# Premultiplied q and k weights in chunks of six whole heads, each matrix transposed in six transfers

## The chip, the cores and the metric

The kernel runs on one NeuronCore of a Trainium2 chip. The core has TensorE (PE: matrix multiply, writing to the eight banks of PSUM), VectorE (DVE), ScalarE (ACT), GpSimd (POOL) and SyncE (SP, here only a queue that starts DMAs). The engines run side by side, each through its own queue in order, and wait for each other through semaphores. The metric is the device time of one execution in microseconds (us), as the median of several runs.

## The reference

For 2,048 tokens of width 640 it computes a gated mixture of two branches of the same input x. Branch A is a linear attention with 32 heads of 20 features, where softmax feature maps stand in for the attention matrix; branch B is a SwiGLU feed-forward network with 1,728 hidden features.

```
g = sigmoid((x * gate_w).sum(-1, keepdims=True))
q, k, v = heads of x @ wqkv
pq = einsum("bhsd,hdf->bhsf", q, w_phi)      # pk the same from k
phi_q = concat([softmax(pq), softmax(-pq)])  # phi_k the same from pk
kv = einsum("bhsf,bhsd->bhfd", phi_k, v)
z = einsum("bhsf->bhf", phi_k)
a = (einsum("bhqf,bhfd->bhqd", phi_q, kv) / (einsum("bhqf,bhf->bhq", phi_q, z) + 1e-6)) @ wo
b = (silu(x @ w_gate) * (x @ w_up)) @ w_down
out = g * a + (1 - g) * b
```

All inputs are bfloat16.

## The kernel before

Since pq = (x @ wq) @ w_phi head by head, the kernel multiplies the weights first: it forms wq' = wq @ blockdiag(w_phi) and wk' likewise, two matrices of 640 x 640, once per execution. After that each tile of 128 tokens needs one product with wq' or wk' (tile `wqk`) instead of two.

This premultiplication is what the change touches. For the matmul, the weights must lie with their output features on the partitions, so a DMA transpose brings the q and the k part of `A_wqkv` into SBUF transposed, as tile `wqT` (`load_wT`, one transfer for each matrix). w_phi is loaded into `wph`, and POOL builds the block diagonal matrices `wbd` out of it (`build_wbd`: a copy repeated for each head, then two selections that clear what lies off the diagonal blocks). `premult` then takes five groups for each matrix, one for each 128 rows of the result: six matmuls, an eviction by ACT or DVE into `wqk`. The 640 columns are cut into five chunks of 128 there, and as 128 is not a multiple of 20, a head can straddle two chunks. A chunk covers all heads that it touches (`PHI_H0`, `PHI_NH`: 7, 7, 8, 7 and 7 heads, 720 columns for 640), the straddling heads are summed in PSUM, and the middle chunk is cut in two, so that each half of the result fills 320 columns of its own bank.

The order of the work is not written out by hand. Every piece of work is a task with an estimated cost, dependences, a priority and sometimes a time before which it may not start. A planner (`_Plan.run`) plays these tasks through when the program is built and so fixes the order on each engine; the chip then executes that order, with real waits on semaphores. Loads have a due time (`land`) in this plan and are chained, so that SP issues them in the order of the source. What reads a load is planned no earlier than its due time (with a slack of 1.0 for the later loads). The order around the change on SP's queue is: x for tokens 512 to 1023, w_phi, a piece of the gate and of the up weights, the transposed k weights, another piece of both, the v weights, x for tokens 1024 to 1535, two more pieces of both, x for the last 512 tokens, the transposed q weights, then w_down and wo. On TensorE, the first tiles of the FFN come first; the groups for k are spread between FFN tiles from 24 us on, the value products (`vtile`) and key products (`ktile`) of the first tokens follow, and the groups for q lie between FFN work from 45 us on. In the later part, FFN, query tiles (`qtile`) and the down projection are interleaved.

Of the kernel before, what the change touches and what calls it, by code (L numbers as in the profile page):

```python
# [6 lines left out]
P = 128  # L7
S_TOK = 2048
D = 640
H = 32  # L10
DH = 20
F_FFN = 1728
# [10 lines left out]
OW = HP * DH  # L23
KV_G = (0, 6, NG)

PHI_H0 = (0, 6, 12, 19, 25)
PHI_NH = (7, 7, 8, 7, 7)
ACTF = mybir.ActivationFunctionType
ALU = mybir.AluOpType
AX = mybir.AxisListType  # L30
# [1 line left out]
BF16 = DT.bfloat16  # L32
# [204 lines left out]
class _Plan:  # L237
# [11 lines left out]
    def add(self, eng, cost, fn, deps=(), prio=5.0, lat=None, acq=(), rel=(), name=""):  # L249
        t = _Task(eng, cost, fn, deps, prio, self.LAT[eng] if lat is None else lat,  # L250
                  tuple(acq), tuple(rel), len(self.tasks), name)
        self.tasks.append(t)
        return t
# [86 lines left out]
def _build(  # L340
# [13 lines left out]
    pe, act, dve, pool, sp = nc.tensor, nc.scalar, nc.vector, nc.gpsimd, nc.sync  # L354
# [13 lines left out]
    def sbat(name, shape, dtype, at):  # L368
        t = nc.alloc_sbuf_tensor_at(name, list(shape), dtype, offset=at)
        tr.reg_tensor(t, "sbuf", at, rowelems(shape), mybir.dt.size(dtype))  # L370
        return t

    xT = sb("xT", [P, 5, S_TOK], BF16)
    wqk = sb("wqk", [P, 2, 5, D], BF16)
    wvg = sb("wvg", [P, 5, D + 1], BF16)
    wo = sb("wo", [P, 5, D], BF16)
    wd = sb("wd", [P, NK, D], BF16)
    wg = sb("wg", [P, 5, F_FFN + 64], BF16)
# [24 lines left out]
    base = nc.lookup_mloc(slab).addr  # L403
    assert base % 32 == 0, base
    xsb = sbat("xsb", [P, NT, D], BF16, base)
    wqT = sbat("wqT", [P, 10, D], BF16, base)
    wbd = sbat("wbd", [P, 5, 8, DH], BF16, base + 10 * D * 2)
    wph = sbat("wph", [P, 5, DH], BF16, base + 10 * D * 2 + 5 * 8 * DH * 2)

    ps = nc.alloc_psum_tensor("ps", [P, 8 * 512], F32)  # L410
    tr.addr[ps.name] = ("psum", 0, 8 * 512, 4)
# [5 lines left out]
    add = plan.add  # L417

    def bank(i, j, c0, c1, r0=0, r1=P):
        return ps[r0:r1, (2 * i + j) * 512 + c0:(2 * i + j) * 512 + c1]  # L420
# [4 lines left out]
    def wide(i, n=D):  # L425
        return ps[:, 2 * i * 512:2 * i * 512 + n]

    def mms(groups):

        reads = [g[1] for g in groups] + [g[2] for g in groups]  # L430
        writes = []
        seen = set()
        for g in groups:
            k = (g[0].offset, str(g[0].ap))
            if k not in seen:
                seen.add(k)
                writes.append(g[0])

        def fn():
            last = None  # L440
            for o, l, r, st, sp_ in groups:
                last = pe.matmul(o, lhsT=l, rhs=r, start=st, stop=sp_, skip_group_check=True)  # L442
            return last
        run("pe", fn, reads=reads, writes=writes)
# [12 lines left out]
    def poolop(fn, reads, writes):  # L457
        run("pool", fn, reads=reads, writes=writes)

    def memset(t_ap, val, eng):  # L460
        eobj = {"pool": pool, "dve": dve}[eng]
        run(eng, lambda: eobj.memset(t_ap, val), reads=[], writes=[t_ap])
# [23 lines left out]
    def load(eng, dst, src, land, prio, transpose=False, name="load", cost=0.06):  # L486

        t = add(eng, cost, lambda: dma(eng, dst, src, transpose=transpose), prio=prio, lat=2.0, name=name)
        t.land = land
        t.slack = L_SLACK if land > 13 else 0.0  # L490
        t.after = chain.get(eng)
        chain[eng] = t
        return t

    def rows(a):
        return a.rearrange("(c p) j -> p c j", p=P)
    gsrc = rows(B_w_gate)
    usrc = rows(B_w_up)
    PIECES = ((0, 512), (512, 768), (768, 1024), (1024, 1344), (1344, 1664))
    NPC = len(PIECES)  # L500
    wgl = [None] * (NPC + 1)
    wul = [None] * (NPC + 1)

    def load_gu(j, eng, land, prio):
        c0, c1 = PIECES[j]
        wgl[j] = load(eng, wg[:, :, c0:c1], gsrc[:, :, c0:c1], land[0], prio)
        wul[j] = load(eng, wu[:, :, c0:c1], usrc[:, :, c0:c1], land[1], prio + 0.1)

    def load_x(bt, prio, *cuts):

        tok = slice(512 * bt, 512 * bt + 512)
        out_ = []
        for i, (c0, c1, land) in enumerate(cuts):
            out_ += [load("sp", xT[:, c0:c1, tok], x2[tok, c0 * P:c1 * P], land, prio + 0.1 * i, True, "x%d" % bt)] * (c1 - c0)
        return out_

    def load_wT(which, land, prio):
        o = 5 * which
        return load("sp", wqT[:, o:o + 5, :], A_wqkv[:, which * D:(which + 1) * D], land, prio, True, "wT")

    gate_ap = bass.AP(gate_w.tensor, gate_w.offset, [[1, P], [P, 5], [1, 1]])

# [5 lines left out]
    xs = [None] * NBT  # L528
# [3 lines left out]
    def load_head(key, c0, c1, k0, k1, land, prio):  # L532
        w, src = (wg, gsrc) if key == "g" else (wu, usrc)
        t = load("sp", w[:, c0:c1, k0 * P:k1 * P], src[:, c0:c1, k0 * P:k1 * P], land, prio)
        for k in range(k0, k1):
# [8 lines left out]
    wul[0] = load_head("u", 2, 5, 0, HD, 11.3, -39)  # L544
    load_gu(1, "sp", (12.5, 13.7), -37)
    xs[1] = load_x(1, -36.5, (0, 5, 16.4))
    ph_l = load("sp", wph[:, :, :], rows(A_w_phi.rearrange("h e f -> (h e) f")), 16.5, -36.2)
    load_gu(2, "sp", (17.6, 18.8), -36)
    wkT_l = load_wT(1, 21.6, -34)
    load_gu(3, "sp", (23.2, 24.8), -33)  # L550
    wv_l = load("sp", wvg[:, :, 0:D], rows(A_wqkv[:, 2 * D:3 * D]), 27.3, -32)
    xs[2] = load_x(2, -31, (0, 5, 31.0))
    load_gu(4, "sp", (32.4, 33.9), -30)
    wgl[NPC] = load("sp", wg[:, :, 1664:1728], gsrc[:, :, 1664:1728], 34.2, -29)
    wul[NPC] = load("sp", wg[:, :, 1728:1792], usrc[:, :, 1664:1728], 34.6, -28)
    xs[3] = load_x(3, -27, (0, 5, 37.4))
    wqT_l = load_wT(0, 41.5, -26)
    wd_l = [load("sp", wd[:, 0:13, :], rows(B_w_down[0:13 * P, :]), 48.5, -25),
            load("sp", wd[0:64, 13, :], B_w_down[13 * P:F_FFN, :], 49.0, -24)]
    wo_l = load("sp", wo[:, :, :], rows(A_wo), 51.0, -23)  # L560
    xl = [x_[4] for x_ in xs]


# [8 lines left out]

    def build_wbd(c):
        nh = PHI_NH[c]
        d_ = wbd[:, c, 0:nh, :]
        s_ = wph[:, c, :].unsqueeze(1).to_broadcast([P, nh, DH])
        poolop(lambda: pool.tensor_copy(d_, s_), [wph[:, c, :]], [d_])
        poolop(lambda: pool.affine_select(
            out=d_, in_=d_, pattern=[[-DH, nh], [0, DH]], compare_op=ALU.is_ge, fill=0.0,
            base=P * c - DH * PHI_H0[c], channel_multiplier=1), [d_], [d_])  # L580
        poolop(lambda: pool.affine_select(
            out=d_, in_=d_, pattern=[[DH, nh], [0, DH]], compare_op=ALU.is_gt, fill=0.0,
            base=DH * PHI_H0[c] + DH - P * c, channel_multiplier=-1), [d_], [d_])
    wbd_t = [add("pool", 1.2, lambda c=c: build_wbd(c), deps=[ph_l], prio=-5, name="wbd") for c in range(5)]

    def build_mask(i):
        d_ = places(kvm[:, :])[:, :, i, :]
# [116 lines left out]
            ffn_tail(0, k, cs[k], (last["g", k], last["u", k]), 0)  # L704

    B_FIRST = 8
    K_AT, K_EACH, Q_AT, Q_EACH = 30.0, 6.08, 120.8, 8.05
    PRE_Q = 10.06
    PRE_EACH = 2.2
    PRE_AT = 23.6  # L710
    D_AFTER = 4
    FIN_DVE = 12
    K_PAIRS = 9
    store_t = {}
# [64 lines left out]
    def premult(which, wT_l, prio, step=0.0, at=0.0):  # L779
        ev = []  # L780
        for m in range(5):
            ctx = {}

            def fn(m=m, ctx=ctx):
                i = ctx["ps"]
                l = [wqT[:, 5 * which + c, P * m:P * m + P] for c in range(5)]

                def r(c, k0, k1):
                    return wbd[:, c, k0:k1, :].rearrange("p k f -> p (k f)")
                mms([(bank(i, 0, 0, 140), l[0], r(0, 0, 7), True, False),  # L790
                     (bank(i, 0, 120, 260), l[1], r(1, 0, 7), False, False),
                     (bank(i, 0, 240, 320), l[2], r(2, 0, 4), False, True),
                     (bank(i, 1, 0, 80), l[2], r(2, 4, 8), True, False),
                     (bank(i, 1, 60, 200), l[3], r(3, 0, 7), False, False),
                     (bank(i, 1, 180, 320), l[4], r(4, 0, 7), False, True)])
            t1 = add("pe", 0.4, fn, deps=[wT_l] + wbd_t, prio=prio + step * m, acq=[("pair", ctx, "ps")], name="pre")
            t1.hold = at + PRE_EACH * m if at else 0.0

            def ev_fn(m=m, ctx=ctx):
                i_ = wide(ctx["ps"], 1024).rearrange("p (b x) -> p b x", b=2)[:, :, 0:320]  # L800
                o_ = wqk[:, which, m, :].rearrange("p (b x) -> p b x", b=2)
                if which and m % 2:
                    dveop(lambda: dve.tensor_copy(o_, i_), [i_], [o_])
                else:
                    actop(o_, i_, ACTF.Copy)
            ev.append(add("dve" if which and m % 2 else "act", 0.73 if which and m % 2 else 0.6, ev_fn, deps=[t1], prio=-1,
                          rel=[("pair", ctx, "ps")], name="prev"))
        return ev
# [218 lines left out]
    for bt in range(1, NBT):  # L1027
        ks = list(range(K_PAIRS if bt == 1 else 0, NK))
        ds = [("d", u, bt - 1) for u in range(4)]
        for i, k in enumerate(ks):  # L1030
            seq.append(("f", k, bt))
            if i >= D_AFTER and ds:
                seq.append(ds.pop(0))
# [67 lines left out]
```

## Time and profile before

| | |
|---|---|
| median of 3 runs | 287.46 us (287.23 to 287.61) |
| profiled execution, first to last instruction | 285.6 us |
| TensorE busy | 282.2 us, 99% |
| TensorE's waits after its first matmul of the FFN | none shown |
| DVE busy | 223.9 us, 78% |
| POOL busy | 171.2 us, 60% |
| ACT busy | 146.2 us, 51% |
| share of 16 DMA engines that SP's queue took | 38.5%, most of it in the first 52 us |
| premultiplication on TensorE | 60 matmuls, between 24.6 and 75.7 us |
| building the block diagonals on POOL | 15 operations, 17.6 to 23.0 us |

Times of a view are counted from the first instruction, so they end at 285.6 and not at the median. An instruction's duration reaches from its start to its end, and successive matmuls overlap; what a row of matmuls costs TensorE is the distance between starts. SP's rows are the time that its queue took to issue a DMA; the data land later.

### The profile page before, as it was taken

What the parts mean: (1) busy time and instruction counts of PE and PEld (TensorE: products, weight loads), DVE (VectorE), ACT (ScalarE), POOL (GpSimd) and SP (SyncE); (2) the same over time, 40 slices, a digit from 0 to 9 for tenths busy, and PEclk for the clock granted to TensorE, in tenths of its full rate; (3) what the DMA queues carried; (4) which work ended last, traced back from release to release, by engine and by line L of the source; (5) the groups of instructions that cost most, each with busy time, mean ns of one, the idle gap of its engine ahead of it and who ended that gap; (6) DMA issues with size and microseconds to landing.
All of it is one profiled execution on the core that took longest, in us unless ns stands there. A gap on an engine that the chain in (4) does not pass through costs nothing.

```text
span 285.6 us, 5119 instructions
## 1 busy us (share of the span) xinstructions
PE 282.2 (99%) x2050; PEld 151.0 (53%) x2050; DVE 223.9 (78%) x318; ACT 146.2 (51%) x222; POOL 171.2 (60%) x164
## 2 busy tenths in 40 slices
PE   8999999999999999999999999999999999999996
PEld 3445555455555555655445555555455565545654
DVE  1324299999999999999999977989999978970312
ACT  2555656775756584344563454456655545564110
POOL 5199407686388748663684577676986666665100
DMA  7999999200000000000217517363435335323211
GB/s 178 258 234 268 225 187 330 88 1 1 2 0 2 0 0 2 2 0 0 45 20 82 127 50 143 75 95 76 93 79 96 67 66 117 60 39 75 69 48 46
DMA packets 65848, 23.91 MB, mean 84 GB/s; under 512 B 53984, under 2 KB 65824, under 8 KB 65824
## 3 DMA queue, kind: packets, MB, share of 16 engines
q1 hardware_dynamic: 65168, 23.58, 38.5%
q8 instruction: 16, 0.26, 0.4%
q10 hardware_dynamic: 656, 0.00, 0.1%
q14 instruction: 8, 0.07, 0.1%
HBM read 8.30 MB, written 2.62 MB: 38 GB/s over the span
## 4 chain that ended last, share of the span: by engine, by line
PE 97%; DMA 1%; SPq 0%; DVE 0%; issue 0%
PE ps L442 97%; DMA xT<-in_A_x_dram 1%; SPq L470 0%; DVE xsb L738 0%
## 5 line engine op out<-in xcount | busy, mean ns | idle before, releaser
L905 POOL TENSOR_TENSOR phi<-phi,rc 128x1320 bf16<-128x1320 bf16 x32 | 77.6, 2426 | 37.8 <-DVE rc L899 37.7
L654 POOL TENSOR_TENSOR hT<-hT,us 128x512 bf16<-128x512 bf16 (+1 forms) x56 | 64.1, 1154 | 41.8 <-DVE hT L648 21.2
L442 PE MATMUL ps<-xT,wg 128*128 128x512 bf16 x280 | 69.1, 379 | 0.2 <-DMA xT<-in_A_x_dram 0.2
L442 PE MATMUL ps<-xT,wu 128*128 128x512 bf16 x260 | 64.3, 379 | 0.0
L442 PE MATMUL ps<-wd,hT 128*128 128x512 bf16 (+1 forms) x448 | 63.0, 299 | 0.0
L648 DVE SCALAR_TENSOR_TENSOR hT<-hT,ps 128x512 bf16<-128x512 bf16 (+1 forms) x56 | 37.5, 674 | 20.4 <-ACT hT L452 20.4
L895 DVE TENSOR_REDUCE sm<-phi 128x66 f32<-128x1320 bf16 x32 | 48.5, 1517 | 6.2 <-ACT phi L452 6.0
L452 ACT ACTIVATE phi<-phi 128x1320 bf16<-128x1320 bf16 x32 | 41.6, 1301 | 17.9 <-DVE phi L884 17.6
L452 ACT ACTIVATE hT<-ps 128x512 bf16<-128x512 f32 (+1 forms) x56 | 33.1, 594 | 34.1 <-PE ps L442 33.6
L442 PEld LDWEIGHTS ps<-wd,hT 128*128 128x128 bf16 x448 | 35.0, 98 | 26.9
L442 PE MATMUL ps<-wqk,xT 128*128 128x512 bf16 (+1 forms) x320 | 48.5, 299 | 0.0
L452 ACT ACTIVATE us<-ps 128x512 bf16<-128x512 f32 (+1 forms) x56 | 33.2, 597 | 17.2 <-PE ps L442 15.7
L442 PEld LDWEIGHTS ps<-xT,wu 128*128 128x128 bf16 x260 | 25.3, 98 | 30.9 <-issue 0.3
L442 PEld LDWEIGHTS ps<-xT,wg 128*128 128x128 bf16 x280 | 25.7, 98 | 25.9 <-issue 0.8
L442 PEld LDWEIGHTS ps<-wqk,xT 128*128 128x128 bf16 x320 | 26.2, 98 | 21.2 <-ACT hT L452 0.2
L872 DVE TENSOR_REDUCE mx<-ps 128x33 f32<-128x660 f32 x32 | 26.8, 837 | 9.3 <-PE ps L442 9.2
L452 ACT ACTIVATE xsb<-ps,gs 128x640 bf16<-128x640 f32 x16 | 12.7, 795 | 32.3 <-PE ps L442 32.3
L884 DVE TENSOR_TENSOR phi<-mn,ps 128x660 bf16<-128x660 f32 x32 | 26.3, 821 | 0.4
L880 DVE TENSOR_TENSOR phi<-ps,mx 128x660 bf16<-128x660 f32 x32 | 26.3, 821 | 0.0
L876 DVE TENSOR_REDUCE mn<-ps 128x33 f32<-128x660 f32 x32 | 26.2, 819 | 0.0
L752 POOL TENSOR_TENSOR xsb<-xsb,xb 128x640 bf16<-128x640 bf16 x12 | 16.7, 1395 | 14.3 <-ACT xb L452 14.3
L442 PE MATMUL ps<-wo,oT 128*128 128x512 bf16 (+1 forms) x160 | 24.3, 299 | 0.0
(44 smaller groups left out, 187.9 us busy)
## 6 DMA issues: line engine op xcount, KB each, us to landing
out_dram<-xsb SPq DMA_DIRECT2D x15, 160.0 KB, 2.0
wd<-in_B_w_down_dram SPq DMA_DIRECT2D x1, 2080.0 KB, 9.4
wg<-in_B_w_gate_dram SPq DMA_DIRECT2D x2, 400.0 KB, 4.1
wu<-in_B_w_up_dram SPq DMA_DIRECT2D x2, 400.0 KB, 4.9
wvg<-in_A_wqkv_dram SPq DMA_DIRECT2D x1, 800.0 KB, 6.9
wo<-in_A_wo_dram SPq DMA_DIRECT2D x1, 800.0 KB, 10.7
wg<-in_B_w_gate_dram SPq DMA_DIRECT2D x2, 320.0 KB, 4.2
wu<-in_B_w_up_dram SPq DMA_DIRECT2D x2, 320.0 KB, 4.8
```

What stands on the lines that cost most here:

```text
L442: last = pe.matmul(o, lhsT=l, rhs=r, start=st, stop=sp_, skip_group_check=True)
L452: run("act", lambda: act.activation(o, i, func, scale=scale), reads=reads, writes=[o])
L648: dveop(lambda: dve.scalar_tensor_tensor(out=hap, in0=hap, scalar=1.0, in1=g_, op0=ALU.add, op1=ALU.mult), [hap, g_], [hap])
L654: poolop(lambda: pool.tensor_tensor(hap, hap, u_, ALU.mult), [hap, u_], [hap])
L752: poolop(lambda: pool.tensor_tensor(x_, x_, b_, ALU.add), [x_, b_], [x_])
L872: dveop(lambda: dve.tensor_reduce(a, b, AX.X, ALU.max), [b], [a])
L876: dveop(lambda: dve.tensor_reduce(a, b, AX.X, ALU.min), [b], [a])
L880: dveop(lambda: dve.tensor_tensor(o_, a, b, ALU.subtract), [a, mx[:, ctx["st"], :]], [o_])
L884: dveop(lambda: dve.tensor_tensor(o_, a, b, ALU.subtract), [b, mn[:, ctx["st"], :]], [o_])
L895: dveop(lambda: dve.tensor_reduce(a, b, AX.X, ALU.add), [b], [a])
L905: poolop(lambda: pool.tensor_tensor(a, a, b, ALU.mult), [a, r], [a])
```

## The change

The columns are cut into chunks of 120, which are six whole heads: five of these and a sixth of 40 columns, two heads. No head straddles two chunks any more, so nothing is summed in PSUM and the six matmuls of a group write 120, 120, 120, 120, 120 and 40 columns next to each other. They start at column 32 of the first bank, so that the fourth piece ends with the bank. The full chunks use 120 rows of the weights; the last uses 128, with zeros in `wbd` below its 40 rows. A chunk of 120 columns isn't what one transfer of the whole matrix gives, so each matrix is now transposed by six transfers of 128 columns that begin 120 columns apart; w_phi comes in two loads. `build_wbd` makes six chunks and first clears the last one. The planner's due times behind these loads move by 1.0 to 2.0 us, and a few of its constants get other values, so the order that it makes differs in places on every engine; the loads on SP's queue keep theirs.

```diff
-PHI_H0 = (0, 6, 12, 19, 25)
-PHI_NH = (7, 7, 8, 7, 7)
+PC = 6 * DH
+NPC_W = 6
+PHI_NH = (6, 6, 6, 6, 6, 2)
...
     def load_wT(which, land, prio):
-        o = 5 * which
-        return load("sp", wqT[:, o:o + 5, :], A_wqkv[:, which * D:(which + 1) * D], land, prio, True, "wT")
+        o = NPC_W * which
+        col = [which * D + PC * c for c in range(NPC_W)]
+        return [load("sp", wqT[:, o + c, :], A_wqkv[:, col[c]:col[c] + P], land - 1.0 * (NPC_W - 1 - c), prio + 0.01 * c, True, "wT") for c in range(NPC_W)]
...
-    ph_l = load("sp", wph[:, :, :], rows(A_w_phi.rearrange("h e f -> (h e) f")), 16.5, -36.2)
+    phi_rows = A_w_phi.rearrange("h e f -> (h e) f")
+    ph_l = [load("sp", wph[:, 0:5, :], phi_rows[0:5 * PC, :].rearrange("(c p) j -> p c j", p=PC), 16.5, -36.2),
+            load("sp", wph[0:2 * DH, 5, :], phi_rows[5 * PC:D, :], 16.6, -36.1)]
     load_gu(2, "sp", (17.6, 18.8), -36)
-    wkT_l = load_wT(1, 21.6, -34)
-    load_gu(3, "sp", (23.2, 24.8), -33)
-    wv_l = load("sp", wvg[:, :, 0:D], rows(A_wqkv[:, 2 * D:3 * D]), 27.3, -32)
-    xs[2] = load_x(2, -31, (0, 5, 31.0))
...
-    wqT_l = load_wT(0, 41.5, -26)
...
+    wkT_l = load_wT(1, 22.6, -34)
+    load_gu(3, "sp", (24.2, 25.8), -33)
+    wv_l = load("sp", wvg[:, :, 0:D], rows(A_wqkv[:, 2 * D:3 * D]), 28.3, -32)
+    xs[2] = load_x(2, -31, (0, 5, 32.0))
...
+    wqT_l = load_wT(0, 43.5, -26)
...
     def build_wbd(c):
         nh = PHI_NH[c]
-        d_ = wbd[:, c, 0:nh, :]
-        s_ = wph[:, c, :].unsqueeze(1).to_broadcast([P, nh, DH])
-        poolop(lambda: pool.tensor_copy(d_, s_), [wph[:, c, :]], [d_])
+        n = nh * DH
+        if n < PC:
+            memset(wbd[:, c, 0:nh, :], 0.0, "pool")
+        d_ = wbd[0:n, c, 0:nh, :]
+        s_ = wph[0:n, c, :].unsqueeze(1).to_broadcast([n, nh, DH])
+        poolop(lambda: pool.tensor_copy(d_, s_), [wph[0:n, c, :]], [d_])
...
-    wbd_t = [add("pool", 1.2, lambda c=c: build_wbd(c), deps=[ph_l], prio=-5, name="wbd") for c in range(5)]
+    wbd_t = [add("pool", 1.0, lambda c=c: build_wbd(c), deps=ph_l, prio=-5, name="wbd") for c in range(NPC_W)]
...
-    K_AT, K_EACH, Q_AT, Q_EACH = 30.0, 6.08, 120.8, 8.05
+    K_AT, K_EACH, Q_AT, Q_EACH = 30.0, 6.098, 120.51, 7.998
     PRE_Q = 10.06
-    PRE_EACH = 2.2
+    PRE_EACH = 2.1
     PRE_AT = 23.6
-    D_AFTER = 4
+    D_AFTER = 3
...
-                l = [wqT[:, 5 * which + c, P * m:P * m + P] for c in range(5)]
-
-                def r(c, k0, k1):
-                    return wbd[:, c, k0:k1, :].rearrange("p k f -> p (k f)")
-                mms([(bank(i, 0, 0, 140), l[0], r(0, 0, 7), True, False),
-                     (bank(i, 0, 120, 260), l[1], r(1, 0, 7), False, False),
-                     (bank(i, 0, 240, 320), l[2], r(2, 0, 4), False, True),
-                     (bank(i, 1, 0, 80), l[2], r(2, 4, 8), True, False),
-                     (bank(i, 1, 60, 200), l[3], r(3, 0, 7), False, False),
-                     (bank(i, 1, 180, 320), l[4], r(4, 0, 7), False, True)])
-            t1 = add("pe", 0.4, fn, deps=[wT_l] + wbd_t, prio=prio + step * m, acq=[("pair", ctx, "ps")], name="pre")
+                def piece(c, o_, n):
+                    k_ = PC if n == PC else P
+                    return (o_, wqT[0:k_, NPC_W * which + c, P * m:P * m + P],
+                            wbd[0:k_, c, 0:n // DH, :].rearrange("p k f -> p (k f)"), True, True)
+                mms([piece(c, bank(i, 0, 32 + PC * c, 32 + PC * c + PC), PC) for c in range(4)] +
+                    [piece(4, bank(i, 1, 0, PC), PC), piece(5, bank(i, 1, PC, PC + 2 * DH), 2 * DH)])
+            t1 = add("pe", 0.285, fn, deps=wT_l + wbd_t, prio=prio + step * m, acq=[("pair", ctx, "ps")], name="pre")
...
-                i_ = wide(ctx["ps"], 1024).rearrange("p (b x) -> p b x", b=2)[:, :, 0:320]
-                o_ = wqk[:, which, m, :].rearrange("p (b x) -> p b x", b=2)
+                i_ = wide(ctx["ps"], 32 + D)[:, 32:32 + D]
+                o_ = wqk[:, which, m, :]
```

More of the change, by code (lines that the diff above doesn't have):

```diff
@@ L405, in _build @@
     xsb = sbat("xsb", [P, NT, D], BF16, base)
-    wqT = sbat("wqT", [P, 10, D], BF16, base)
-    wbd = sbat("wbd", [P, 5, 8, DH], BF16, base + 10 * D * 2)
-    wph = sbat("wph", [P, 5, DH], BF16, base + 10 * D * 2 + 5 * 8 * DH * 2)
+    wqT = sbat("wqT", [P, 2 * NPC_W, D], BF16, base)
+    wbd = sbat("wbd", [P, NPC_W, 6, DH], BF16, base + 2 * NPC_W * D * 2)
+    wph = sbat("wph", [PC, NPC_W, DH], BF16, base + 2 * NPC_W * D * 2 + NPC_W * 6 * DH * 2)
     ps = nc.alloc_psum_tensor("ps", [P, 8 * 512], F32)
@@ L546, in _build @@
     xs[1] = load_x(1, -36.5, (0, 5, 16.4))
-    ph_l = load("sp", wph[:, :, :], rows(A_w_phi.rearrange("h e f -> (h e) f")), 16.5, -36.2)
+    phi_rows = A_w_phi.rearrange("h e f -> (h e) f")
+    ph_l = [load("sp", wph[:, 0:5, :], phi_rows[0:5 * PC, :].rearrange("(c p) j -> p c j", p=PC), 16.5, -36.2),
+            load("sp", wph[0:2 * DH, 5, :], phi_rows[5 * PC:D, :], 16.6, -36.1)]
     load_gu(2, "sp", (17.6, 18.8), -36)
-    wkT_l = load_wT(1, 21.6, -34)
-    load_gu(3, "sp", (23.2, 24.8), -33)
-    wv_l = load("sp", wvg[:, :, 0:D], rows(A_wqkv[:, 2 * D:3 * D]), 27.3, -32)
-    xs[2] = load_x(2, -31, (0, 5, 31.0))
[L553 to L556, printed above, removed]
-    wqT_l = load_wT(0, 41.5, -26)
-    wd_l = [load("sp", wd[:, 0:13, :], rows(B_w_down[0:13 * P, :]), 48.5, -25),
-            load("sp", wd[0:64, 13, :], B_w_down[13 * P:F_FFN, :], 49.0, -24)]
-    wo_l = load("sp", wo[:, :, :], rows(A_wo), 51.0, -23)
+    wkT_l = load_wT(1, 22.6, -34)
+    load_gu(3, "sp", (24.2, 25.8), -33)
+    wv_l = load("sp", wvg[:, :, 0:D], rows(A_wqkv[:, 2 * D:3 * D]), 28.3, -32)
+    xs[2] = load_x(2, -31, (0, 5, 32.0))
+    load_gu(4, "sp", (33.4, 34.9), -30)
+    wgl[NPC] = load("sp", wg[:, :, 1664:1728], gsrc[:, :, 1664:1728], 35.2, -29)
+    wul[NPC] = load("sp", wg[:, :, 1728:1792], usrc[:, :, 1664:1728], 35.6, -28)
+    xs[3] = load_x(3, -27, (0, 5, 38.4))
+    wqT_l = load_wT(0, 43.5, -26)
+    wd_l = [load("sp", wd[:, 0:13, :], rows(B_w_down[0:13 * P, :]), 50.5, -25),
+            load("sp", wd[0:64, 13, :], B_w_down[13 * P:F_FFN, :], 51.0, -24)]
+    wo_l = load("sp", wo[:, :, :], rows(A_wo), 53.0, -23)
     xl = [x_[4] for x_ in xs]
@@ L574, in build_wbd @@
         nh = PHI_NH[c]
-        d_ = wbd[:, c, 0:nh, :]
-        s_ = wph[:, c, :].unsqueeze(1).to_broadcast([P, nh, DH])
-        poolop(lambda: pool.tensor_copy(d_, s_), [wph[:, c, :]], [d_])
+        n = nh * DH
[4 more added lines that the diff above has]
+        poolop(lambda: pool.tensor_copy(d_, s_), [wph[0:n, c, :]], [d_])
         poolop(lambda: pool.affine_select(
             out=d_, in_=d_, pattern=[[-DH, nh], [0, DH]], compare_op=ALU.is_ge, fill=0.0,
-            base=P * c - DH * PHI_H0[c], channel_multiplier=1), [d_], [d_])
+            base=0, channel_multiplier=1), [d_], [d_])
         poolop(lambda: pool.affine_select(
             out=d_, in_=d_, pattern=[[DH, nh], [0, DH]], compare_op=ALU.is_gt, fill=0.0,
-            base=DH * PHI_H0[c] + DH - P * c, channel_multiplier=-1), [d_], [d_])
-    wbd_t = [add("pool", 1.2, lambda c=c: build_wbd(c), deps=[ph_l], prio=-5, name="wbd") for c in range(5)]
+            base=DH, channel_multiplier=-1), [d_], [d_])
+    wbd_t = [add("pool", 1.0, lambda c=c: build_wbd(c), deps=ph_l, prio=-5, name="wbd") for c in range(NPC_W)]
     def build_mask(i):
```

## The prediction

> **What bounds the kernel now.** I read the chain of waits first, then the groups by shape, then the two timelines that the change meets: TensorE's, and that of SP's queue, which issues every load. The chain:
>
> ```profile
> 1.32 3.72 DMA xT<-in_A_x_dram
> 5.17 278.13 PE ps L442 x2040
> 283.33 0.35 DVE xsb L738
> ```
>
> From the first landing to the last matmul the chain is TensorE alone, 2,040 matmuls without a wait. So two things can move the time: matmul columns, one for one, and any new wait of TensorE, also one for one, since a queue that never idles has nothing to give it back with. That DVE, ACT and POOL are busy 78%, 51% and 60% of the span says nothing here. The matmuls that change, and where they stand:
>
> ```profile
> L442 PE MATMUL ps<-wbd,wqT 128*128 128x140 bf16 x40 | 4.6, 224 | 0.0
> L442 PE MATMUL ps<-wbd,wqT 128*128 128x80 bf16 x20 | 2.4, 200 | 0.0
> 24.59 0.48 PE L442 MATMUL ps<-wbd,wqT 128*128 128x140 bf16 x6
> 24.91 1.24 PE L442 MATMUL ps<-xT,wg 128*128 128x512 bf16 x5
> 25.99 1.24 PE L442 MATMUL ps<-xT,wu 128*128 128x512 bf16 x5
> 30.17 1.03 PE L442 MATMUL ps<-wvg,xT 128*128 128x512 bf16 x4
> 45.49 0.48 PE L442 MATMUL ps<-wbd,wqT 128*128 128x140 bf16 x6
> ```
>
> The durations (224, 200 ns) overlap; what a group costs is the distance to the next start. Five matmuls of 512 columns take 25.99 - 24.91 = 1.08 us, 216 ns each, or 0.417 ns a column and some 2.7 ns each. A premultiplying group takes 24.91 - 24.59 = 0.32 us; by the same rate its 4 x 140 + 2 x 80 = 720 columns give 0.300 + 0.016 = 0.316. The other lines give the moments that TensorE needs three loads: the transposed k weights at 24.59, the v weights at 30.17, the transposed q weights at 45.49. Now SP's queue, and what its transposes take to issue:
>
> ```profile
> 1.32 1.32 SPq L470 DMA_TRANSPOSE xT<-in_A_x_dram  x1
> 3.82 2.53 SPq L470 DMA_TRANSPOSE xT<-in_A_x_dram  x2
> 13.50 0.58 SPq L470 DMA_DIRECT2D wph<-in_A_w_phi_dram  x1
> 15.27 4.73 SPq L470 DMA_TRANSPOSE wqT<-in_A_wqkv_dram  x1
> 20.04 0.58 SPq L470 DMA_DIRECT2D wg<-in_B_w_gate_dram  x1
> 21.23 0.53 SPq L470 DMA_DIRECT2D wvg<-in_A_wqkv_dram  x1
> 21.80 7.59 SPq L470 DMA_TRANSPOSE xT<-in_A_x_dram  x1
> 35.74 5.16 SPq L470 DMA_TRANSPOSE wqT<-in_A_wqkv_dram  x1
> L470 SPq DMA_TRANSPOSE eT<-phi x16: 1264/1387/1451, 140.1 to 257.8; - x16
> L470 SPq DMA_TRANSPOSE oT<-ob x16: 1199/1207/1584, 149.8 to 268.3; - x16
> ```
>
> Count a transpose in blocks of 128 x 128. The first of x has 8 blocks and takes 1.32 us to issue, the next two 8 and 4 and take 2.53 together, oT has 5 and takes 1.21, eT 11 and takes 1.39. So up to 11 blocks the issue costs some 1.2 to 1.3 us whatever the size. The big ones, 25 blocks of the weights in 4.73 and 5.16, cost 0.19 to 0.21 a block. A chunk of the change is 640 x 128, 5 blocks: it belongs with the small ones. Landings, from issue (transposed weights, then v weights with the gate column, then oT; smallest, median, largest):
>
> ```profile
> DMA to landing us min/median/max: 6.8/7.0/7.2
> DMA to landing us min/median/max: 6.1/6.5/6.9
> DMA to landing us min/median/max: 2.6/2.6/4.3
> ```
>
> The k weights thus land at 15.27 + 7.2 = 22.5 at the latest, 2.1 us ahead of their use; the v weights (the 6.9; the gate column is the 6.1) at 21.23 + 6.9 = 28.13, 2.0 ahead; the q weights at 35.74 + 7.2 = 42.9, 2.5 ahead. These three margins are what the change spends from.
>
> **Matmul columns: a gain of 0.25 us.** A group becomes 5 x 120 + 40 = 640 columns: 80 fewer, 33 ns, if the matmul of 40 columns streams at the same rate. No row has one so short; the nearest, 176 of 64 columns, follow each other every 29 ns. With 29 for it the gain is 23 ns. I take 25; ten groups give 0.25 (0.23 to 0.33). Weights of 120 rows stand in no row either. All loads here take 95 to 99 ns and hide even behind matmuls of 64 columns, and the load still has 128 columns, so I take no change; if short rows cost the full 98 ns each, five per group would add (98 - 53) x 50 = 2.2 us, which I keep for the range only.
>
> **SP's queue: 3.66 us later behind the k weights.** The second load of w_phi costs what the first does, 0.58 and a gap of 0.05: the first chunk is issued at 15.27 + 0.63 = 15.90. Six chunks at 1.25 + 0.05 end at 15.90 + 7.80 = 23.70, where one transpose ended and the next load began at 20.04: 3.66 later. With 1.207 a chunk it is 3.4, with 1.32 it is 4.1. The planner of the changed kernel allows 1.0 for it.
>
> **First wait, the k weights.** The sixth chunk is issued at 15.90 + 5 x 1.30 = 22.40 and, like oT with its 5 blocks, lands 2.6 later, at 25.0. TensorE comes at 24.59 (nothing ahead of it changes) and waits some 0.5, with the 0.14 that the chain shows from the first landing to the first matmul (0.3 to 1.0). All of TensorE is queued behind, and so is ACT, which waits for its banks.
>
> **Second wait, the v weights, which decides.** Between the k chunks and the v load stand two unchanged loads, so its issue slips to 21.23 + 3.66 = 24.89 and its landing, 6.9 later, to 31.79. Four groups shorter by 0.025 stand ahead, so TensorE would be there at 30.07. It starts at 31.79 + 0.14 = 31.93: 1.86 lost, the first wait included, not beside it. With the bounds of the issue 1.6 to 2.3.
>
> **Third wait, the q weights.** The transpose of x that follows the v load took 7.59 to issue. The DMA engines stood nearly still in the middle of it (share 0.01 and 0.09 in the two half microseconds from 28.5), so 1.4 of it may not return, as its packets now come behind the v weights. The six q chunks start 2.2 to 3.7 late, at 37.9 to 39.4; the sixth lands 6.5 + 2.6 later, at 47.0 to 48.5. The groups ahead are the same as before in number, so TensorE comes at 45.49 - 0.12 + 1.86 = 47.23: nothing to 1.4 more. I take nothing. The loads behind (w_down, wo) are first used after 105 us, far off.
>
> **POOL and the rest.** Building the block diagonals takes 17.57 to 23.04, 1.09 us a chunk. Three operations of 120 columns instead of 140 save some 0.06 (a chunk of 160 columns cost 64 ns more than one of 140), and there is a sixth chunk with a memset: about 0.65 us more, done at 23.7 against 24.6. The margin of 0.9 covers it; behind it are four products of the FFN, 0.65 late, and POOL's idle 0.41 at 28.0 takes most of that up. Uncovered it would cost at most 0.65, and the first wait above would hide most of that. The eviction still has 640 columns (696 ns on ACT, 824 on DVE): nothing.
>
> **Sum.** 1.86 - 0.25 = +1.6 us: a span of 285.6 becomes 287.2. The median of the runs, 287.46, is 1.9 above the profiled span, launch and end; the same on top gives 289.1.
>
> The Trainium skill, page DMA: Bandwidth & Descriptors, section Issuing engines are not separate DMA queues, says that the sequencer's time to start a DMA is usually small next to the DMA itself. That speaks for the first rival below and against the rows of oT and of x.
>
> **Rivals.** (1) Issue goes by blocks, not by transfers: at 4.73 / 25 = 0.19 a block, 30 blocks take 5.7. With five gaps and the w_phi load SP is 1.8 late, the v weights land at 29.96, and TensorE waits 30.10 - 30.07 = 0.03. Then only the columns count: 287.2. It speaks for it that the big transposes go so; against it, that 5, 8 and 11 blocks cost nearly the same. It decides from 1.8 us of delay down. (2) The halt of the DMA engines at 28.5 returns, on the v weights: 1.4 more, 290.5. For it: it came twice (again from 39.0); against: both times a transpose was in flight. (3) The new due times put the later work in another order on every engine (TensorE's rows are 484 where they were 499). DVE is 9 tenths busy in most slices from 50 to 200 us; a wait of 0.06 in each of 16 query tiles gives 290.1. For it: those slices; against: before, TensorE never waited under the same load. (4) The 120-row loads of the bound above: 291.3.
>
> **Chances.** Forecast 0.70, (1) 0.13, (2) 0.07, (3) 0.08, (4) 0.02. A measurement of this kernel tells 0.2%, 0.6 us, from no change. Cases (2) to (4) and nearly all of the forecast are slower; (1) lies mostly within 0.2%, a quarter of it faster. That makes faster 0.04, same 0.11, slower 0.85. The forecast's own range is 288.4 to 289.9 (issue bounds, the third wait in part). I go to 287.8 and 290.5, which leaves out (1), (4) and tails, less than 2 in 10.
>
> **What will show it.** In the profile after: six issues of 1.2 to 1.3 us for each matrix in SP's queue, and the next load at about 23.7; TensorE waiting on the k weights near 24.6 and on the v weights near 30.6, 1.9 in total, in the chain as DMA; next to none at 47; premultiplying groups 0.29 apart. Chunks issued in 0.95 or less would make the forecast wrong, and so would v weights that land before 30.1, or waits of TensorE on DVE or ACT late in the span.

## The result and the profile after

The changed kernel takes 291.78 us, the median of 5 runs (291.44 to 293.06). The kernel before took 287.61 on the same chip (5 runs, 287.23 to 287.98). The ratio is 1.0156, 95% interval 1.0142 to 1.0169: 4.5 us slower by the means of the runs, 4.2 by their medians, where 1.6 was forecast. The forecast named the right direction, and 291.78 lies above its range of 287.8 to 290.5. The profiled execution took 292.56 us, with a span of 290.8 and a mean granted clock of TensorE of 0.994; of the five runs two were such (spans 290.8 and 291.3), and three had a clock of 1.000 and spans of 289.7 to 290.1. One run of all that follow, of the kernel with v and q both early, took 572.28 us at a mean clock of 0.877; it counts in the median given there, but not in the ratio.

The end of the chain of waits after (start and length in us, what ran or was waited for):

```profile
22.12 1.27 SPq L471
...
24.64 8.81 DMA wvg<-in_A_wqkv_dram
33.45 0.05 issue
33.50 17.14 PE ps L443 x116
50.63 0.16 issue
50.80 237.68 PE ps L443 x1790
```

The chain no longer begins with the first tokens. It goes through SP's queue and the v weights, and TensorE starts on them at 33.50. It breaks once more at 50.80, where TensorE takes up the first group of the q weights. From there on it is TensorE alone, as before. TensorE's timeline at the three gates (start, us, engine, line, operation, count, idle time before and what ended it):

```profile
23.39 1.24 PE L443 MATMUL ps<-xT,wu 128*128 128x512 bf16 x5
25.66 0.44 PE L443 MATMUL ps<-wbd,wqT 120*128 120x120 bf16 x6 [1.02 <-DMA wqT<-in_A_wqkv_dram]
25.95 1.24 PE L443 MATMUL ps<-xT,wg 128*128 128x512 bf16 x5
...
33.50 4.58 PE L443 MATMUL ps<-wvg,xT 128*128 128x512 bf16 x20 [2.21 <-DMA wvg<-in_A_wqkv_dram]
37.91 0.45 PE L443 MATMUL ps<-wbd,wqT 120*128 120x120 bf16 x6
...
49.10 1.53 PE L443 MATMUL ps<-wvg,xT 128*128 128x512 bf16 x10
50.80 0.44 PE L443 MATMUL ps<-wbd,wqT 120*128 120x120 bf16 x6 [0.16 <-issue]
```

Against the starts of before (24.59, 30.17, 45.49) TensorE is 1.07 late at the k weights, 3.33 late at the v weights and 5.31 late at the q weights; the last group of matmuls starts at 280.69 instead of 275.52, 5.17 late. So all of the loss is there by 51 us, and nothing behind it adds to it. Three parts make the 5.31: the waits of 1.02 and 2.21; 1.67 between 33.50 and 37.91, where 20 matmuls on the v weights take 4.41 us and took 32.91 - 30.17 = 2.74 before; and 0.33 at 50.80, as that group would follow the start at 49.10 by 1.37 (after the same work at 38.20 the next starts at 39.57). That is 5.23 of it. The row at 50.80 names no load, but the sixth q chunk, issued at 47.4, landed 3.2 us later, at 50.6. The last part is small only because the first two have already used up the time to that landing; the experiments below show it. SP's queue after:

```profile
13.50 1.06 SPq L471 DMA_DIRECT2D wph<-in_A_w_phi_dram  x2
...
15.61 7.79 SPq L471 DMA_TRANSPOSE wqT<-in_A_wqkv_dram  x6
23.44 0.58 SPq L471 DMA_DIRECT2D wg<-in_B_w_gate_dram  x1
...
24.64 0.53 SPq L471 DMA_DIRECT2D wvg<-in_A_wqkv_dram  x1
25.21 8.45 SPq L471 DMA_TRANSPOSE xT<-in_A_x_dram  x1
...
39.91 8.72 SPq L471 DMA_TRANSPOSE wqT<-in_A_wqkv_dram  x6
```

The six issues for k take 7.79 us where one took 4.73, and the load behind them starts at 23.44 instead of 20.04. The six for q take 8.72 where one took 5.16, and they start 4.17 late. The rows of tile `wqT` in after (issue times in ns, smallest, median, largest; then from issue to landing):

```profile
L471 SPq DMA_TRANSPOSE wqT<-in_A_wqkv_dram x12: 1218/1271/2160, 15.6 to 47.4; - x12
...
DMA to landing us min/median/max: 3.2/3.9/4.9
```

The chunks are issued in the time of the small transposes (the median is 1.27 us, one took 2.16), but land later than oT's 2.6. The v weights, by the chain, need 8.8 us instead of 6.9. What happens meanwhile shows in the windows of after (stretch, length, busy time and number of instructions of PE, PEld, DVE, ACT and POOL, granted clock, DMA share, GB/s; the share adds up packets that lie open side by side, so it can pass 1, and GB/s is what moved):

```profile
30.00:31.00 1.00, 1.00 (x14) 0.64 (x12) 0.69 (x1) 0.52 (x2) 1.00 (x2) 1.00 1.95 299
31.00:32.00 1.00, 0.29 (x6) 0.15 (x3) 0.68 (x1) 0.94 (x2) 0.81 (x2) 1.00 2.08 56
32.00:33.00 1.00, 0.00 (x0) 0.00 (x0) 0.15 (x1) 0.00 (x0) 0.64 (x1) 1.00 0.04 4
...
33.50:34.00 0.50, 0.50 (x3) 0.26 (x4) 0.00 (x0) 0.00 (x0) 0.00 (x0) 1.00 1.27 290
...
34.50:35.00 0.50, 0.50 (x4) 0.23 (x3) 0.00 (x0) 0.00 (x0) 0.00 (x0) 0.50 1.27 290
...
37.00:37.50 0.50, 0.50 (x3) 0.19 (x2) 0.00 (x0) 0.00 (x0) 0.00 (x0) 0.50 1.13 360
...
38.00:39.00 1.00, 1.00 (x12) 0.59 (x10) 0.00 (x0) 0.89 (x2) 0.00 (x0) 1.00 1.32 232
```

Two things are to be seen. From 31 to 33 us the DMA engines move 56 and then 4 GB/s, after 299: a halt such as before had at 28.5 falls on the v weights here, and it is longer. And TensorE's clock, granted in full when it starts again at 33.50, is at half by 34.50 and back in full by 38: the 1.67 us above.

### The profile page after: what moved, and what is told of

Its sections match the earlier page's. It is cut to its first block, busy times and chain, and to the rows that moved or that the text cites. A ratio compares the mean times of both kernels' runs of the same rounds, so it can differ in the third digit from the quotient of the medians.

```text
span 290.8 us, 5158 instructions
## 1 busy us (share of the span) xinstructions
PE 283.9 (98%) x2050; PEld 151.4 (52%) x2050; DVE 224.7 (77%) x318; ACT 146.3 (50%) x222; POOL 171.3 (59%) x168
## 4 chain that ended last, share of the span: by engine, by line
PE 88%; SPq 8%; DMA 3%; issue 0%; DVE 0%
PE ps L443 88%; SPq L471 8%; DMA wvg<-in_A_wqkv_dram 3%; DVE xsb L745 0%
## 5 line engine op out<-in xcount | busy, mean ns | idle before, releaser
L655 DVE SCALAR_TENSOR_TENSOR hT<-hT,ps 128x512 bf16<-128x512 bf16 (+1 forms) x56 | 37.5, 675 | 21.9 <-ACT hT L453 21.9
L443 PE MATMUL ps<-wvg,xT 128*128 128x512 bf16 (+1 forms) x160 | 25.0, 314 | 2.2 <-DMA wvg<-in_A_wqkv_dram 2.2
```

Of the source, the lines that this page charges most:

```text
L655: dveop(lambda: dve.scalar_tensor_tensor(out=hap, in0=hap, scalar=1.0, in1=g_, op0=ALU.add, op1=ALU.mult), [hap, g_], [hap])
```

## The experiments

**The two parts apart.** The first kernel is the one before, with each matrix in six transfers. The sixth goes to a spare buffer that nobody reads, so chunks, matmuls and block diagonals stay as before. (Of each diff the core is shown. Each ratio is to the kernel before, run beside the experiment.)

```diff
-        return load("sp", wqT[:, o:o + 5, :], A_wqkv[:, which * D:(which + 1) * D], land, prio, True, "wT")
+        out_ = [load("sp", wqT[:, o + c, :], A_wqkv[:, which * D + P * c:which * D + P * c + P], land, prio + 0.01 * c, True, "wT") for c in range(5)]
+        load("sp", spare[:, which, :], A_wqkv[:, which * D:which * D + P], land, prio + 0.05, True, "wT")
+        return out_
```

> The kernel before with one thing changed: each matrix is transposed by six transfers of 128 columns, five that are used and a sixth into spare room that nothing reads. Columns, chunks and the order of work are those of before. Theory (the loss is made on SP's queue: six issues of 1.27 us and gaps, then the v weights late, with the halt of the DMA engines near 31 us and the slower clock behind the wait on top): SP is about 3.0 us late behind the k weights, no wait on the k weights themselves (the fifth lands near 24.0), a wait on the v weights of 1 to 3 us, 288.6 to 292 in all. Rival (the loss is made by the shorter matmuls or by the new order of work): the same time as before, 287.5.

Measured: 291.91 us (4 runs, 291.02 to 292.53), ratio 1.0142 (1.0119 to 1.0165). Its timeline of TensorE:

```profile
33.30 4.58 PE L443 MATMUL ps<-wvg,xT 128*128 128x512 bf16 x20 [2.22 <-DMA wvg<-in_A_wqkv_dram]
37.72 0.48 PE L443 MATMUL ps<-wbd,wqT 128*128 128x140 bf16 x6
...
50.53 0.47 PE L443 MATMUL ps<-wbd,wqT 128*128 128x140 bf16 x6
```

It waits as long for v, loses as much at half clock (37.72 - 33.30 = 4.42) and comes to the q weights at nearly the same moment. The transfers alone make the whole loss.

The second is the kernel after, with each matrix in one transfer of five chunks of 128. The sixth matmul of a group reads the fifth chunk, so the premultiplied weights are made of other columns than the reference's; the number and the shapes of TensorE's instructions are those of after.

```diff
-        col = [which * D + PC * c for c in range(NPC_W)]
-        return [load("sp", wqT[:, o + c, :], A_wqkv[:, col[c]:col[c] + P], land - 1.0 * (NPC_W - 1 - c), prio + 0.01 * c, True, "wT") for c in range(NPC_W)]
+        return [load("sp", wqT[:, o:o + 5, :], A_wqkv[:, which * D:(which + 1) * D], land, prio, True, "wT")]
...
-                    return (o_, wqT[0:k_, NPC_W * which + c, P * m:P * m + P],
+                    return (o_, wqT[0:k_, NPC_W * which + min(c, 4), P * m:P * m + P],
```

> The changed kernel with each matrix transposed in one transfer of five chunks of 128 columns, as before; the matmuls keep their 640 columns and 120 rows, and the sixth reads the fifth chunk. So the chunks hold other columns of the q and k weights than the reference's. The order of work of every engine is that of the changed kernel. Theory: no wait of TensorE on a weight load, and what is left is the gain in columns, 0.24 us: 287.2 to 287.4. Rival (the new order of work or the 120-row weights cost the time): above 288.5.

Measured: 287.34 us (10 runs), ratio 0.9987 (0.9978 to 0.9996). The shorter groups gain what their columns are worth (0.25 of 287 us would be 0.9991), and the loads of 120 rows, the sixth chunk on POOL and the later order of the work cost nothing that can be seen.

**One matrix at a time.** Next the kernel before with only k, then with only q in six transfers (the edit of the first kernel, behind a condition).

```diff
+        if which != 1:
+            return [load("sp", wqT[:, o:o + 5, :], A_wqkv[:, which * D:(which + 1) * D], land, prio, True, "wT")]
```

> The kernel before with the k weights alone transposed in six transfers (the sixth into spare room); the q weights in one. Theory: SP is 3.0 late behind the k weights, the v weights land near 33.4 and TensorE loses 3.1 there, and 1.7 more where its clock drops; the q weights land near 47, behind that loss: 290.6 to 292.4. Rival (the split of the q weights is what costs): under 289.

> The kernel before with the q weights alone transposed in six transfers (the sixth into spare room); the k weights in one. Theory: the fifth, the last that is read, is issued at 35.7 + 4 x 1.31 = 41.0 and lands 3.4 later, at 44.4 to 45.3, ahead of TensorE at 45.5: no loss, 287.6 to 288.0. Rival (the six transfers for q cost by themselves): 289 or more.

Measured: k alone 289.65 us (5 runs, 289.37 to 291.93), ratio 1.0083 (1.005 to 1.0116); q alone 287.72, ratio 1.0003 (0.9994 to 1.0013). For k this is 1 us under what the theory expected, for q as expected. The profile of k alone holds just a loss at v:

```profile
32.04 2.90 PE L443 MATMUL ps<-wvg,xT 128*128 128x512 bf16 x20 [1.63 <-DMA wvg<-in_A_wqkv_dram]
34.78 0.48 PE L443 MATMUL ps<-wbd,wqT 128*128 128x140 bf16 x6
...
47.36 0.48 PE L443 MATMUL ps<-wbd,wqT 128*128 128x140 bf16 x6
```

TensorE is 32.04 - 30.17 = 1.87 late at v, runs at full clock afterwards (2.74 to the next group), and is 1.87 late at q, whose weights here come in one transfer and in time. (One of the five runs had a clock of 0.994: the 291.93.) So six transfers for q cost nothing by themselves, those for k about 2 us, and both together 4: the second half of the loss needs both, k's delay of the whole queue and q's own longer issue.

**Which gate sets the time.** If the wait for v decided, the v weights issued ahead of the third gate and up pieces would cure it.

```diff
     wkT_l = load_wT(1, 22.6, -34)
-    load_gu(3, "sp", (24.2, 25.8), -33)
     wv_l = load("sp", wvg[:, :, 0:D], rows(A_wqkv[:, 2 * D:3 * D]), 28.3, -32)
+    load_gu(3, "sp", (24.2, 25.8), -33)
```

> The changed kernel with the v weights issued ahead of the third pieces of the gate and up weights, straight behind the six k chunks; nothing else moves, on any engine. Theory: the v weights are issued at 23.44 and land near 28.9, before TensorE comes to them at 31.1; the wait on the k weights, 1.0 us, stays, and the clock stays at 1.00: 287.5 + 1.1 - 0.25 = 288.3. Rival (a wait on the v weights is not what decides, or the halt of the DMA engines comes whatever is in flight): 290 or more.

Measured: 292.54 us (4 runs, 291.27 to 293.91), ratio 1.0153 (1.0104 to 1.0202). The expectation missed: nothing was gained. TensorE's timeline in this kernel:

```profile
25.60 0.44 PE L443 MATMUL ps<-wbd,wqT 120*128 120x120 bf16 x6 [0.51 <-DMA wqT<-in_A_wqkv_dram]
...
31.08 2.89 PE L443 MATMUL ps<-wvg,xT 128*128 128x512 bf16 x20
...
50.51 0.69 PE L443 MATMUL ps<-wbd,wqT 120*128 120x120 bf16 x6 [3.97 <-DMA wqT<-in_A_wqkv_dram]
54.51 0.45 PE L443 MATMUL ps<-wbd,wqT 120*128 120x120 bf16 x6
```

The wait for v is gone, and TensorE stands 3.97 us before the q weights instead and starts on them at 50.51, as it does at 50.80 in the kernel after and at 50.53 in the first experiment. The q weights are a second gate at the same place; opening the first only moves the loss there. After the idle time the clock drops again (54.51 - 50.51 = 4.00 to the next group, 2.44 in the kernel after).

So the gates were opened in the other two ways: q alone early (its six chunks right behind the v weights; this edit is shown), and v and q both.

```diff
     wv_l = load("sp", wvg[:, :, 0:D], rows(A_wqkv[:, 2 * D:3 * D]), 28.3, -32)
+    wqT_l = load_wT(0, 43.5, -26)
...
     xs[3] = load_x(3, -27, (0, 5, 38.4))
-    wqT_l = load_wT(0, 43.5, -26)
```

> The changed kernel with the six q chunks alone moved, from the end of the loads of x to straight behind the v weights; the pieces of the gate and up weights stay ahead of the v weights. No engine's own order moves. With the changed kernel, e3 (v moved) and e5 (both moved) this makes a square of two gates. Theory (q is the gate that sets the time of the changed kernel, v stands ahead of it and by itself costs what e7 showed, 2.0 in most runs): 287.6 + 2.0 - 0.2 = 289.4 where the clock stays at 1.00, 291 where it drops. Rival (v is the gate that sets the time, and the q chunks only follow): as the changed kernel, 291.4 to 291.8.

> The changed kernel with the loads in another order on SP: behind the six k chunks come the v weights, then the six q chunks, then the FFN pieces and x as before among themselves. No engine's own order moves. Theory, mended (the v weights and the q weights are two gates in a row; opening the first alone leaves the second, where the sixth q chunk landed at 50.4 to 50.7 in three kernels): v lands near 29.4, the sixth q chunk near 35.5, ten us ahead of its use; only the wait on the k weights stays, 0.5 to 1.0: 287.7 + 0.8 - 0.3 = 288.2, clock 1.00. Rival (a third gate stands behind the two, or the late loads behind it pass the loss on): 290 or more.

Measured: q early 289.59 us (4 runs), ratio 1.0063 (1.0048 to 1.0078); both early 287.97, ratio 1.0011 (1.0000 to 1.0022). As expected for both. With q early TensorE still waits for k and v, and no longer for q:

```profile
25.74 0.45 PE L443 MATMUL ps<-wbd,wqT 120*128 120x120 bf16 x6 [0.82 <-DMA wqT<-in_A_wqkv_dram]
...
32.66 2.91 PE L443 MATMUL ps<-wvg,xT 128*128 128x512 bf16 x19 [1.28 <-DMA wvg<-in_A_wqkv_dram]
...
47.96 0.45 PE L443 MATMUL ps<-wbd,wqT 120*128 120x120 bf16 x6
```

Put as a square: neither early 1.0156, v alone 1.0153, q alone 1.0063, both 1.0011. Opening q is worth 0.9%, opening v nothing while q is shut and 0.5% once q is open. These kernels also differ in how many of their runs lost time at half clock. At a clock of 0.999 or more the spans are 289.7 to 290.1 us with neither early, 289.5 to 289.6 with v, 287.6 to 288.1 with q and 286.0 to 287.1 with both, so the order doesn't rest on the clock. The q gate sets the time of the changed kernel, and the v gate is the next below it.

**The halt of the DMA engines.** To see whether the transpose of x that is in flight behind the v weights makes the halt, it was moved behind four pieces of the gate and up weights.

```diff
-    xs[2] = load_x(2, -31, (0, 5, 32.0))
     load_gu(4, "sp", (33.4, 34.9), -30)
...
+    xs[2] = load_x(2, -31, (0, 5, 32.0))
     xs[3] = load_x(3, -27, (0, 5, 38.4))
```

> The changed kernel with the transposed load of x for tokens 1024 to 1535 issued behind the four FFN pieces that followed it; nothing else moves. So no transpose is in the DMA queue when the v weights land. Theory (the halt of the DMA engines near 31 us needs a transpose in flight): the v weights land 6.7 to 6.9 us after their issue at 24.64, near 31.4, TensorE loses 1.3 in the two waits and keeps its clock: 288.5. Rival (the halt comes with the fetch of instructions near 30.5, whatever is in flight): the v weights land 8.8 us after their issue, 291 or more.

Measured: 293.14 us (4 runs, 291.55 to 294.68), ratio 1.0186 (1.0139 to 1.0233); the expectation missed. A window of this kernel, with the columns as above:

```profile
29.70:31.00 1.30, 1.30 (x16) 0.83 (x15) 0.69 (x1) 0.82 (x2) 1.30 (x2) 1.00 1.07 362
```

And its TensorE at the two gates:

```profile
32.87 2.90 PE L443 MATMUL ps<-wvg,xT 128*128 128x512 bf16 x20 [1.65 <-DMA wvg<-in_A_wqkv_dram]
...
50.52 0.44 PE L443 MATMUL ps<-wbd,wqT 120*128 120x120 bf16 x6 [2.18 <-DMA wqT<-in_A_wqkv_dram]
...
54.65 0.45 PE L443 MATMUL ps<-wbd,wqT 120*128 120x120 bf16 x6
```

There is no halt here (362 GB/s, and 351 and 347 in the next two microseconds), and yet the v weights need 8.0 us to land. Probably the plain loads that are now behind them share the DMA engines with them; no run shows that by itself. So this run doesn't give the halt's price. And the q weights still open at 50.5. The clock drops here too, at q (54.65 - 50.52 = 4.13 to the next group instead of 2.44), in the profile; the two runs at full clock took 291.55 and 292.33 us, about the time of the changed kernel.

**No wait at all.** Two kernels take the late landings as given. One is the kernel with v and q early, with the k groups held back to 25.2 in the plan; it was run twice, in separate sets.

```diff
-    PRE_AT = 23.6
+    PRE_AT = 25.2
```

> The kernel of e5 with one planner constant changed as well: the first k group may start no earlier than 25.2 in the plan instead of 23.6, so that one more gate and up tile of the FFN stands ahead of it. Theory: TensorE comes to the k weights at 26.8, behind the landing of the sixth chunk at 25.6, and waits for no load; the gain in columns alone is left: 287.3, below the kernel before. Rival (the new order makes a wait of its own, or the k wait was no loss): 288 or more.

> The kernel of e6 once more, in five rounds, beside the kernel before. Theory (ten groups shorter by 0.025 us and no wait): 0.25 us below the kernel before, a ratio of 0.9991. Rival (the loads' order has a cost of its own that eats the gain): 1.000 or above.

Measured: 287.28 us, ratio 0.9991 (0.9982 to 1.0000), then 287.66, ratio 0.9999 (0.9990 to 1.0009). The loss is gone; that the 0.25 us of the columns are kept can't be told from these.

The other leaves the loads of the changed kernel in their own order and form and only tells the planner when they land on the chip, so that it puts other work first on TensorE.

```diff
-    wkT_l = load_wT(1, 22.6, -34)
-    load_gu(3, "sp", (24.2, 25.8), -33)
-    wv_l = load("sp", wvg[:, :, 0:D], rows(A_wqkv[:, 2 * D:3 * D]), 28.3, -32)
+    wkT_l = load_wT(1, 24.6, -34)
+    load_gu(3, "sp", (27.4, 28.9), -33)
+    wv_l = load("sp", wvg[:, :, 0:D], rows(A_wqkv[:, 2 * D:3 * D]), 32.6, -32)
...
-    wqT_l = load_wT(0, 43.5, -26)
+    wqT_l = load_wT(0, 49.8, -26)
...
-    PRE_AT = 23.6
+    PRE_AT = 25.2
```

> The changed kernel with its loads in its own order and form, and the planner's due times set to the landings that the changed kernel's trace showed: the k weights 25.6, the v weights 33.6, the q weights 50.8, the others in step; the first k group no earlier than 25.2. The planner then puts FFN tiles ahead of the weights' first uses. With no wait TensorE would come to k at 26.8, to v at 34.7 and to q at 51.0. Theory (the loss is TensorE standing at loads that the plan takes for landed; the late landing by itself costs nothing): no wait on a load, 287.3 to 288.0. Rival (six transfers cost time whatever the plan knows of them): 290 or more.

Measured: 287.17 us (10 runs, 286.84 to 288.04), ratio 0.9985 (0.9973 to 0.9998): 4.6 us less than the changed kernel, and the shortest median of all that were run. SP's queue in it:

```profile
15.62 7.86 SPq L471 DMA_TRANSPOSE wqT<-in_A_wqkv_dram  x6
...
39.11 8.60 SPq L471 DMA_TRANSPOSE wqT<-in_A_wqkv_dram  x6
```

And TensorE's timeline in it:

```profile
27.69 0.45 PE L443 MATMUL ps<-wbd,wqT 120*128 120x120 bf16 x6
...
35.63 1.53 PE L443 MATMUL ps<-wvg,xT 128*128 128x512 bf16 x10
...
51.98 0.74 PE L443 MATMUL ps<-wbd,wqT 120*128 120x120 bf16 x12
```

The transposes are issued as slowly as in the changed kernel, and no row of TensorE waits for a weight load any more: FFN work and other tiles lie ahead of each gate. In this kernel the twelve issues are free as long as nothing is planned before they have landed.

## Why the prediction was right, and where it failed

**Right: SP's queue.** Six issues were forecast at 1.25 + 0.05 each, 7.80 in all, and took 7.79 for k and 8.72 for q; the queue behind k is 23.44 - 20.04 = 3.40 late, forecast 3.66 (bounds 3.4 to 4.1). Rival 1, issue by blocks, wanted 5.7 and falls. (One reading was a little low: eT, with 11 blocks, takes 1.39, not 1.2 to 1.3. The chunks, with 5 blocks, don't rest on it.) The Trainium skill (page DMA: Bandwidth & Descriptors, section Issuing engines are not separate DMA queues) says that the time to start a DMA is usually small next to the DMA itself. The traces here do not bear that out for these chunks: the issue of one takes 1.27 us, a third of the 3.9 to its landing, and six in a row delay everything behind them.

**Right: the columns, POOL and the order.** A premultiplying group takes 25.95 - 25.66 = 0.29, loads of 120 rows take 95 to 100 ns, the block diagonals were done at 23.6 (forecast 23.7), ahead of TensorE, and the kernel that leaves out only the split transfers is not slower. Rivals 3 and 4 fall with that.

**Mis-sized: the first wait.** Forecast 0.5 (0.3 to 1.0), measured 1.02. The landing was taken from oT's 2.6, and the chunks, with as many blocks, took 3.2 to 4.9.

**Mis-sized: the second wait.** With the v weights issued at 24.89 and landing 6.9 later, TensorE was to lose 1.86. They were issued a little earlier, 24.64, and landed 8.8 later, with the halt in between, and TensorE was 3.33 late there. Rival 2 named this halt, at 290.5 and with a chance of 0.07, which was little for something that the profile of before showed twice. With k alone split the loss was 1.87, just the forecast size, but by luck: there the v weights were issued at 24.27, 0.6 earlier than forecast, and took 7.7 us to land, 0.8 more than forecast.

**Failed: the third wait.** "nothing to 1.4 more. I take nothing." This is the step that broke the forecast, and with it the name "which decides" for the second: the square shows that q sets the time. With the q gate opened and the other waits left, the kernel took 289.59 us, inside the forecast's range; with the v gate opened and q left, it took 292.54. The lower end of the range, the sixth chunk landing at 47.0, was taken, and each of its terms was too small. The q chunks start at 39.91, not 37.9 (this end let the transpose of x ahead of them issue in 6.2 us, 7.59 less the halt's 1.4, and it took 8.45: + 2.0). The sixth is issued 47.4 - 39.9 = 7.5 later, not 6.5 (one issue took 2.16 us: + 1.0). It lands 3.2 after that, not 2.6 (+ 0.6). Together 47.0 + 3.6 = 50.6. The upper end, 48.5, kept the 7.59 for x, but had no slow issue and no landing slower than oT's in it, so it was too early as well. Against the 47.23 at which the forecast has TensorE come to q, a landing at 50.6 is a wait of 3.4 us in place of nothing; with v opened TensorE stood 3.97 us there.

**Not foreseen: the clock.** That an idle TensorE can be given half its clock afterwards was in no term. In the profile it costs 1.67 us at v, but it probably did not add to the whole in full: TensorE would have reached the q weights earlier and waited there, as the three runs at full clock suggest with spans only some 1 us shorter. There is no trace of one of those, so this is argued, not shown.

## What to carry to other kernels

Cutting one large DMA transpose into pieces cost its queue 1.27 us of issue for each piece here (the median), and what counts is what stands behind it in that queue, gate by gate: work out the landing of every load behind, not only of the next one, for an earlier gate that is opened passes its loss to the next. Where a consumer's order is planned, give the plan the landings that a trace shows; that cured all of the loss here without touching a transfer.

## What the runs showed of the hardware

**A halt of the DMA engines.** The halt of 31 to 33 us begins just after an instruction fetch, which is seen among the DMA queues from 30.5 us (after, 30 to 34 us: queue, kind, packets, MB, share):

```profile
q1 hardware_dynamic: 1521, 0.53, 119.2%
q8 instruction: 1, 0.02, 3.2%
```

But the fetch isn't needed. With the due times taken from the trace, the traffic falls in the same way, and from 28 to 33 us no instruction queue is listed (its window from 31 to 32 us, and all queues from 28 to 33):

```profile
31.00:32.00 1.00, 1.00 (x6) 0.43 (x5) 0.45 (x1) 0.62 (x1) 1.00 (x2) 1.00 0.30 36
q1 hardware_dynamic: 1913, 1.14, 117.8%
```

The same holds for the falls near 30 us with the columns alone and near 32 us with q early, both to about 20 GB/s without a fetch in the 2 us ahead. With q early a fetch at 28.0 us, with q chunks in flight, brought no fall in the 2.5 us behind it (over 260 GB/s). What these falls share is a transpose in flight; with plain loads alone, as in the kernel with x moved back, a fetch brought none (362 GB/s). This is a pattern seen, not one that an experiment isolated, and the cause stays open.

**The clock after a short idle time.** Idle gaps of 2.21 (after, at v), 2.22 (both matrices split, at v), 2.18 (x moved back, at q) and 3.97 us (v early, at q) were each followed by 3.4 us at a granted clock of 0.50, worked out from windows of half a microsecond (in after 0.87 from 34.0, 0.50 from 34.5 to 37.5, 0.71 to 38.0). With v early the drop began some 0.2 us before the gap ended, in the others after it. In the profiles, gaps of 1.28 (q early), 1.63 (k alone split) and 1.65 us (x moved back, at v) were not; whether the same gap brings the drop in every run no trace shows. The Trainium skill (page TensorE: Matmul & The Clock Gate, section Why this matters for your kernels) warns of gaps of more than about 3 us; here 2.2 us was enough. The Trainium skill, on the same page, section What's actually happening, knows only a half and a full clock. The windows bear that out: they show 0.50 and 1.00, and values between them only where the clock changes inside a window.
